# A recurrent attention loop: the attention mask copied into the score banks by ScalarE, and tail work moved within the tile

## The chip, the cores and the metric

The kernel runs on one core of one Trainium2 chip. It is one launch that computes a transformer block and its whole backward pass. The metric is the device time in microseconds (us). Three runs of the kernel before took 3000.04, 2988.55 and 2992.74 us, median 2992.74.

The engines are named as in the profile: PE (TensorE, matmuls and transposes), DVE (VectorE), ACT (ScalarE), POOL (GpSimd), SP (SyncE, which here issues most of the DMAs). L790 is line 790 of the kernel before. Matmul results land in PSUM; everything else lives in SBUF.

## The reference

The forward part, with a sequence of 2048 rows, D = 512, 32 heads of width 128, segments of 32 rows and a memory of 8 rows:

```python
mod = (silu(c) @ w_mod)                       # sa, ca, ga, sb, cb, gb
h = layernorm(x) * (1 + ca) + sa
mem = mem0
for s in range(64):                           # 64 segments
    hs = concat([mem, h[32*s : 32*s+32]])     # 8 + 32 = 40 rows
    q, k, v = hs @ Wq, hs @ Wk, hs @ Wv       # per head
    scores = q @ k.T * scale
    scores = where(mask, scores, -1e9)        # memory rows are seen by all, the rest is causal
    o = softmax(scores) @ v @ Wo
    mem = o[:8]                               # the next segment's memory
    outs.append(o[8:])
x = x + ga * concat(outs)
h = layernorm(x) * (1 + cb) + sb
out = x + gb * ((sigmoid(h @ w_gate) * (h @ w_up)) @ w_down)
```

The outputs are `out` and, for a given `grad_out`, the gradients of x, mem0, Wq, Wk, Wv, Wo, w_gate, w_up, w_down, c and w_mod. Because `mem` of one segment is an input of the next, the 64 segments can only run one after the other.

## The kernel before

The kernel has phases: a short phase 0 (modulation vectors, weights loaded), phase 2 (layernorm and the recurrent attention, from about 18.6 to 970 us), then the gated unit, the attention's backward pass and the weight gradients. The change touches phase 0 and phase 2 only, in the function `phase2` with its helpers.

**Tiling.** Four segments (s4 = 0, 1, 2, 3) make a tile of 128 rows; there are 16 tiles. The 40 rows of a segment are 8 memory rows and 24 rows in one 32-row block, and the remaining 8 rows, the *tail rows*. These do not need the memory to be projected, so the tail rows of all four segments are projected together, a tile ahead. Heads are kept in 11 groups of three (120 columns a group: 3 x 40). The groups are worked in three parts (`NP` = 3) of 4, 4 and 3 groups, that is 480, 480 and 360 columns.

**One segment**, in the order in which PE runs it:

1. Key and query passes of the 32-row block (`proj`, two halves each), value pass (`v_chunk`), with the transposes `turns` that bring rows to head columns.
2. `st_exp(0..2)`: the score matmuls of a part accumulate into a bank `st_ps` that already holds the mask (`start=False`); ScalarE's Exp (L850) reads it and writes ET. The mask is written there at the end of the segment before by `mask_mm` (L786, matmul at L790): a matmul of the identity with `maskT`, which has the mask already repeated for each group. There are three `st` banks, one for each part.
3. `den` (L854) and `recip` (L859) give the softmax's denominators; `pv` (L874) multiplies ET with the values into `or_ps`; `ost` scales the result into Ost: part 0 by VectorE in one instruction (L898), part 1 by ScalarE in four (L895), part 2 by VectorE.
4. `ott(0..2)`: transposes (L866) of Ost into `tps`, copied to OT (L61 ACT, L63 DVE): part 0 by VectorE, parts 1 and 2 by ScalarE.
5. `outproj` (`pair_mm`, L223): 64 matmuls of OT with Wo into `at_ps`, head pairs in order; `split_pair` (L230 ACT, L232 DVE) makes a high and a low bf16 half, `sum_pair` (L242) folds both into `at_ft`, and ScalarE copies the memory rows to `hT_next` (L1046). With that the next segment starts.

**Work laid into the segment.** The order of instructions on every engine in phase 2 is fixed as written: `pin(i0)` chains all instructions of an engine. So each `fill`, `p1`, `chunk` or `pop_later` call stands where it is called:

- `p1(j, k)`: step k of the layernorm of tile j, two tiles ahead: load L395, stats L398, scale L409, shift L414, turn L419. The turn is four transposes into `p1tp`, a copy by ScalarE (hx, L424) and one by GpSimd (hb, L426). Before: stats at the end of the projection of s4 = 0, scale at s4 = 1, shift at s4 = 2, turn at s4 = 3 between den(2) and pv(2).
- `b_pieces`: projection of the next tile's tail rows (`proj_b`, with stores `rows_out`), `turn_b` (L630, eight transposes, at the place "turn" of s4 = 2 for k and s4 = 3 for q, ahead of `ott(0)`). Its copies out of PSUM wait in the list `evacs` until `evac_turned`, after the output projection.
- `TailRows` (object `tail`): output projection of the tail rows of the tile before, 32 heads in pieces of sizes (24, 8), both at s4 = 3 after the projection (`ao_tps`, L215); then `split`, and at s4 = 0 of the next tile the fold (L327) with VectorE's cast `ao_b_tb` (L335), taken by `pop_later` (`early`).
- `store_rows`: for each segment the attention rows `at_ft` are cast (L335), transposed (`at_tp`, L339), copied (`at_rb`, L341) and stored (L345) in the next segment.

PSUM tiles named `or_ps`, `tps`, `turn_ps`, `p1tp`, `at_ps`, `at_tp`, `at_ft`, `ao_tps`, `pass_ps` share five buffers (tag "p").

**The first segment** is different: the weights arrive while it runs, and the output weights Wo come in quarters by SP (`load_wo`, L809). The stores of its rows (`first_stores`: 2 of RA0k, 6 of RBk, 6 of RBq, 2 of RA0q, L597 to L605) are issued by SP after the tail turn of q. Behind them SP issues the two DMA transposes VTr (L978, of the values) and Pst (L986, of ET), then OSR, OT. GpSimd normalizes Pst (L1062).

Of the kernel before, what the change touches and what calls it, by code (L numbers as in the profile page):

```python
# [7 lines left out]
BF16 = mybir.dt.bfloat16  # L8
F32 = mybir.dt.float32
# [31 lines left out]
class K:  # L41
# [336 lines left out]
    def phase1_setup(self, ctx, psum_tile_fn):  # L378
# [11 lines left out]
        def p1_tile(j):  # L390
# [28 lines left out]
            def turn():  # L419
                tp = psum_tile_fn()  # L420
                for c in range(DC):
                    nc.tensor.transpose(tp[:, c, :], st["h1"][:, c * 128:(c + 1) * 128], self.ident[:])
                hx = p1w.tile([128, DC, 128], BF16, name="hx", bufs=3)
                nc.scalar.activation(hx[:], tp[:, 0:DC, :], AF.Copy)  # L424
                hb = p1w.tile([128, DC, nseg, 8], BF16, name="hb", bufs=2)
                nc.gpsimd.tensor_copy(hb[:], hx[:].rearrange("p c (s t) -> p c s t", t=cfg.T)[:, :, :, 24:cfg.T])  # L426
                return hx, hb

# [12 lines left out]
    def phase2(self):  # L441
# [15 lines left out]
        with ExitStack() as ctx:  # L457
# [42 lines left out]

            def p1(j, k=None):
                if j < NT:
                    if j not in p1s:
                        p1s[j] = p1_tile(j)
                    for i in (range(1, 5) if k is None else [k]):
                        r = p1s[j][i]()
                        if r is not None:
                            hxs[j] = r

            p1s = {}  # L510
            mem0 = VTr[0:M, 0:DC, :].rearrange("m c x -> m (c x)")
            with tc.tile_pool(name="p0", bufs=1) as p0:
# [80 lines left out]

            def rows_out(rows, dram, s0, ns):

                if ns == 1:
                    nc.sync.dma_start(dram[s0, 0:96, 0:8, :].rearrange("r g e -> r (g e)"), rows[0:96, 0:1024])  # L597
                    nc.sync.dma_start(dram[s0, 0:96, 8:11, :].rearrange("(hl r) g e -> r hl (g e)", r=32),
                                      rows[96:128, :].rearrange("r (hl x) -> r hl x", hl=3))
                    return  # L600
                for j in range(3):
                    nc.sync.dma_start(dram[s0:s0 + 4, 96 + 8 * j:104 + 8 * j, 0:8, :].rearrange("s q g e -> s q (g e)"),
                                      rows[32 * j:32 * j + 32, 0:1024])
                for hl in range(3):
                    nc.sync.dma_start(dram[s0:s0 + 4, 96 + 8 * hl:104 + 8 * hl, 8:11, :].rearrange("s q g e -> s q (g e)"),  # L605
                                      rows[96:128, 384 * hl:384 * hl + 384])
# [4 lines left out]
            def b_pieces(t):  # L611
# [4 lines left out]
                def proj_b(x, a, n, eng):  # L616
                    hb = hxs[t][1]
                    self.col_pass(psp, Ws[x], 0, lambda c: hb[:, c, :, :].rearrange("p s q -> p (s q)"), RBt[x], eng, steps=(a, n))
                    if a + n == 8:
                        store = lambda: rows_out(RBt[x], DR[x], t * nseg_t, nseg_t)  # L620
                        if t == 0:
                            first_stores.append(store)
                        else:
                            store()

# [22 lines left out]
            def evac_turned():  # L648
                while evacs:
                    evacs.pop(0)()  # L650

            first_stores = []
            firsts = b_pieces(0)
# [127 lines left out]

            tail = TailRows(self, sb2, psp, psp, 1, "ao", rows_b, (24, 8), ptag="p")

            masked = {}

            def mask_mm(pi):  # L786

                n = min(PG, G - pi * PG)
                ps = masked[pi] = pst.tile([128, PG, GW], F32, name="st_ps", tag="st")
                nc.tensor.matmul(ps[:, 0:n, 0:120], lhsT=self.ident[:, :], rhs=maskT[:, 0:n, :], start=True, stop=False,  # L790
                                 skip_group_check=True)

            def tails_in(xs, s):
# [17 lines left out]
            for s in range(NS):  # L811
# [11 lines left out]
                def proj(x, hf, eng):  # L823
                    pass_half(x, hf, lambda c: hT[:, c, :], RA[x], eng)
                    if hf == 1 and s == 0:
                        first_stores.append(lambda: rows_out(RA[x], DR[x], s, 1))
                    elif hf == 1 and s < NS - 1:
                        rows_out(RA[x], DR[x], s, 1)
# [127 lines left out]
                if s == NS - 1:  # L956
# [28 lines left out]
                if s < NS - 1:  # L985
                    nc.sync.dma_start(Pst[:], ET[:, :], transpose=True)  # L986
                else:
                    nc.gpsimd.dma_start(self.w_up, io["B_w_up"].rearrange("(c p) f -> p c f", p=128))
# [1441 lines left out]
```

## Time and profile before

| | |
|---|---|
| runs | 3000.04, 2988.55, 2992.74 us; median 2992.74 |
| profiled execution | 2988.12 us, span 2986.3 us, mean granted PE clock 0.997 |
| busy | PE 2926.4 us (98%), DVE 1629.5, ACT 1270.7, POOL 1234.0 us |
| phase 2 | about 18.6 to 970 us |
| segment 0, segment 1 | 37.16 us, 17.68 us |
| a steady tile | 57.16 us: 14.25 (s4 = 0), 14.02 (1), 14.04 (2), 14.85 (3) |
| windows 300 to 500 us | PE 199.57 of 200 us, DVE 122.87, ACT 115.91, POOL 104.11, granted clock 1.00 |

A segment's length is the time from its first key matmul to that of the next. A PE row of the timeline covers several matmuls ("x7") and may overlap its neighbours, since matmuls are pipelined: the start of a row is the reliable number. "Idle before, releaser" tells what ended an engine's idle time. One granted clock value is the throttle's answer for a stretch: 1.00 is full speed.

### The profile page before, as it was taken

Reading aid. Unit: us, or ns where it says so; the run is one execution under the profiler, and the core shown is the slowest. Engines: PE = TensorE matmul, PEld = TensorE weight load, DVE = VectorE, ACT = ScalarE, POOL = GpSimd, SP = SyncE. Lnnn points to the kernel's source line nnn. Section 1 sums busy time; section 2 is a strip of 40 time slices with the busy share of each in tenths; the row PEclk is TensorE's granted clock in tenths of the full one; section 3 lists DMA queues with packets and bytes.
Section 4 is the critical chain, followed back from the end, with each engine's and each line's share of the span. In section 5 each row is a group of like instructions: output and inputs, shape, how many; then the busy total and the mean of one; then the engine's idle time right before and its main releaser. Section 6 shows DMA issues by size and latency. Waiting matters only on the chain.

```text
span 2986.3 us, 105797 instructions
## 1 busy us (share of the span) xinstructions
PE 2926.4 (98%) x43931; PEld 1837.4 (62%) x44005; DVE 1629.5 (55%) x3680; ACT 1270.7 (43%) x3055; POOL 1234.0 (41%) x2485
## 2 busy tenths in 40 slices
PE   6999999999999999999999999999999999999999
PEld 3666666666666544445577777777777754445455
DVE  5565666666655788833466665566566632840011
ACT  2555555555555533312355555555555520110011
POOL 2455555545555222221244444444444422762111
PEclk9999999999999999999999999999999999999999
DMA  9988889889889899988699999999999997886565
GB/s 307 222 217 218 211 216 224 211 220 215 208 217 274 211 233 231 230 280 281 205 249 251 251 254 246 250 254 249 251 254 252 248 282 246 253 261 191 159 216 171
DMA packets 837924, 703.04 MB, mean 235 GB/s; under 512 B 537682, under 2 KB 709890, under 8 KB 836548
## 3 DMA queue, kind: packets, MB, share of 16 engines
q1 hardware_dynamic: 711828, 485.29, 66.7%
q0 software_dynamic: 54512, 148.63, 15.6%
q10 hardware_dynamic: 71104, 62.34, 6.5%
q8 instruction: 346, 5.67, 0.8%
q14 instruction: 134, 1.10, 0.1%
HBM read 294.99 MB, written 276.35 MB: 191 GB/s over the span
## 4 chain that ended last, share of the span: by engine, by line
PE 91%; DMA 3%; DVE 2%; issue 1%; ACT 1%; SPq 0%; POOL 0%; DVEq 0%; ACTq 0%; POOLq 0%
PE pass_ps L257 14%; PE gps L2211 14%; PE dh_ps L215 8%; PE g_ps L1834 5%; PE pass_ps L666 5%; PE gps5o L2226 4%; PE dhq_ps L223 4%; PE at_ps L223 4%; PE mm L1315 3%; PE gps L1494 3%; PE dh_tps L215 3%; PE turn_ps L838 2%; PE mm L1275 2%; PE mm L1290 2%; PE tps L1751 1%; PE st_ps L848 1%
## 5 line engine op out<-in xcount | busy, mean ns | idle before, releaser
L2211 PE MATMUL gps<-rows,hrows 128*128 128x512 bf16 (+2 forms) x2124 | 413.6, 355 | 1.9
L2211 PEld LDWEIGHTS <-hrows 128*128 128x128 bf16 x2160 | 211.3, 98 | 204.3 <-issue 0.9
L63 DVE CAST ot<-gps 128x512 bf16<-128x512 f32 (+3 forms) x76 | 48.2, 634 | 309.8 <-PE gps L2211 230.4
L1062 POOL TENSOR_TENSOR Pst<-Pst,rden 120x1408 bf16<-120x1408 bf16 x63 | 159.9, 2537 | 116.9 <-issue 66.7
L1879 POOL COPY dOst<-RAd 96x512 bf16<-96x512 bf16 x128 | 75.3, 613 | 295.9 <-DVE RAd L63 295.9
L61 ACT ACTIVATE ot<-gps 128x512 bf16<-128x512 f32 (+3 forms) x75 | 41.2, 550 | 356.8 <-PE gps L2211 214.3
L666 PE MATMUL pass_ps<-Wv,hT 128*32 128x512 bf16 (+2 forms) x2304 | 186.8, 358 | 0.0
L2215 POOL DMA_DIRECT2D out_dram<-ot x104 | 78.7, 757 | 257.0 <-DVE ot L63 133.4
L257 PEld LDWEIGHTS <-hT 128*32 128x32 bf16 x4096 | 114.7, 97 | 98.3 <-issue 4.1
L63 DVE CAST Vst<-pass_ps 96x512 bf16<-96x512 f32 x128 | 87.2, 682 | 107.0 <-ACT RBv L61 98.1
L215 PE MATMUL dh_ps<-WvT,dVT 128*32 128x512 bf16 x2048 | 133.4, 380 | 1.6 <-DVE RBd L63 0.2
L666 PE MATMUL pass_ps<-Wv,hb 128*32 128x512 bf16 (+2 forms) x636 | 127.5, 347 | 2.1 <-DMA Wv<-in_A_Wv_dram 2.1
L223 PE MATMUL at_ps<-Wo,OT 128*32 128x256 bf16 x4096 | 124.7, 274 | 4.1 <-issue 2.1
L257 PE MATMUL pass_ps<-Wk,hT 128*32 128x512 bf16 x2048 | 123.2, 382 | 2.5 <-DVE mv L402 1.1
L257 PE MATMUL pass_ps<-WoT,dyT 128*32 128x256 bf16 (+1 forms) x3072 | 122.4, 308 | 0.9 <-ACT dyT L1960 0.9
L223 PE MATMUL dhq_ps<-WqT,dQT 128*32 128x256 bf16 x4096 | 122.9, 273 | 0.0
L257 PE MATMUL pass_ps<-Wq,hT 128*32 128x512 bf16 x2048 | 122.7, 379 | 0.0
L215 PE MATMUL dh_ps<-WkT,dKT 128*32 128x512 bf16 x2048 | 122.3, 380 | 0.0
L2226 PE MATMUL gps5o<-WoT,rows 128*128 128x512 bf16 x549 | 120.4, 379 | 1.4 <-DMA rows<-OSR 0.9
L801 POOL DMA_DIRECT2D Vst<-RBv x192 | 100.8, 530 | 47.7 <-ACT ET L850 30.7
L223 PEld LDWEIGHTS <-dQT 128*32 128x32 bf16 x4096 | 109.6, 97 | 15.8
L317 DVE TENSOR_TENSOR dST<-dh_ps,dST 128x512 bf16<-128x512 f32 x64 | 44.3, 692 | 130.3 <-ACT dST L316 130.3
(472 smaller groups left out, 7038.6 us busy)
## 6 DMA issues: line engine op xcount, KB each, us to landing
OSR<-Ost SPq DMA_DIRECT2D x64, 352.0 KB
OT<-OT SPq DMA_DIRECT2D x64, 352.0 KB
PS<-Pst SPq DMA_DIRECT2D x64, 352.0 KB
Pst_l<-PS SPq DMA_DIRECT2D x64, 352.0 KB
OT_l<-OT SPq DMA_DIRECT2D x64, 352.0 KB
DVR<-rows_x POOLq DMA_DIRECT2D x64, 352.0 KB, 6.4
DKR<-rows_x POOLq DMA_DIRECT2D x64, 352.0 KB, 5.7
DQR<-rows_x POOLq DMA_DIRECT2D x64, 352.0 KB, 3.5
```

The source lines that it names most:

```text
L63: return nc.vector.tensor_copy(out, in_)
L215: self.nc.tensor.matmul(ps[32 * j:32 * j + 32, :], lhsT=lhsT, rhs=w, start=(n < 4), stop=(n >= total - 4), tile_position=(0, 32 * j))
L223: nc.tensor.matmul(ps[32 * j:32 * j + 32, :], lhsT=x[k], rhs=w[k][:, 256 * d:256 * d + 256], start=(n == 0), stop=(n == total - 1), tile_p ...
L257: self.nc.tensor.matmul(ps[32 * j:32 * j + 32, :], lhsT=lhs(c), rhs=rhs, start=(c == 0), stop=(c == DC - 1), tile_position=(0, 32 * j))
L666: nc.tensor.matmul(ps[32 * j:32 * j + 32, o * E:(o + n) * E], lhsT=lhsT, rhs=wc[:, 3 * a + hl:3 * (a + n - 1) + hl + 1:3, :], start=(c == ...
L801: nc.gpsimd.dma_start(Vst[96 + 8 * j:104 + 8 * j, :], rb[32 * j + o:32 * j + o + 8, :])
L1062: nc.gpsimd.tensor_tensor(Pst[0:120, :, :], Pst[0:120, :, :], rden[:, :].unsqueeze(2).to_broadcast([120, G, 128]), op=ALU.mult)
L1315: nc.tensor.matmul(hp[:], lhsT=xT[:, fc, :], rhs=wT[:, fc, :], start=(n == 0), stop=(n == 2 * FC - 1))
L1494: nc.tensor.matmul(ps[:], lhsT=h2r[:, j, c * 128:(c + 1) * 128], rhs=xr[:, j, :], start=(j == 0), stop=(j == NT - 1))
L1834: nc.tensor.matmul(ps[:, j, 0:w], lhsT=lh[:, g * GW:(g + 1) * GW], rhs=rh[:, g * GW:g * GW + w], start=True, stop=True)
L2211: nc.tensor.matmul(ps[:, 0:ng * E], lhsT=hrows[:, tp_, c * 128:(c + 1) * 128], rhs=rows[:, tp_, 0:ng * E], start=(tp_ == 0), stop=(tp_ == ...
L2226: nc.tensor.matmul(pss[gg][:], lhsT=rows[:, t, gg * E:(gg + 1) * E], rhs=dyrows[:, t, :], start=(n == 0), stop=(n == NTP - 1))
```

## The change

- The mask of parts 0 and 1 is copied into the score banks by ScalarE (`mask_copy`), right after the copy to `hT_next`; part 2 by ScalarE in the next segment, behind the key pass's second copy. The first segment alone keeps `mask_mm`, now over the whole bank. The three `mask_mm` calls in each of the other segments go.
- The layernorm steps of a tile come a segment earlier: scale at s4 = 1 between the two query halves, shift at s4 = 1 after the projection, turn at s4 = 2 after `turn_b` and ahead of `ott(0)`. The two copies of the turn are put into `evacs` and run with `evac_turned` after the projection.
- `pop_later` (the early one, s4 = 0) goes from before `pv(2)` to after `ott(0)`.
- The tail pieces are (8, 16, 8) instead of (24, 8); the first 8 run at s4 = 3 between `ott(0)` and `ott(1)`.
- In the first segment `evac_turned` comes before the query turn; the 12 stores of the tail rows are issued by GpSimd, and the 4 stores of RA0k and RA0q by SP behind the Pst transpose.
- In phase 0 a one-element Exp (`e0`) is run by ScalarE.

```diff
 turn():
-                hx = p1w.tile([128, DC, 128], BF16, name="hx", bufs=3)
-                nc.scalar.activation(hx[:], tp[:, 0:DC, :], AF.Copy)
-                hb = p1w.tile([128, DC, nseg, 8], BF16, name="hb", bufs=2)
-                nc.gpsimd.tensor_copy(hb[:], hx[:]...[:, :, :, 24:cfg.T])
-                return hx, hb
+                def copies():
+                    (the same four lines)
+                    return hx, hb
+                return copies
...
 phase 0
+                nc.scalar.activation(p0.tile([1, 1], F32, name="e0")[:], self.sa_bc[0:1, 0:1], AF.Exp)
...
 proj_b, first tile
-                            first_stores.append(store)
+                            first_stores["b"].append(lambda: rows_out(RBt[x], DR[x], 0, nseg_t, nc.gpsimd))
...
-            tail = TailRows(self, sb2, psp, psp, 1, "ao", rows_b, (24, 8), ptag="p")
+            tail = TailRows(self, sb2, psp, psp, 1, "ao", rows_b, (8, 16, 8), ptag="p")
...
+            def mask_copy(pi):
+                n = min(PG, G - pi * PG)
+                ps = masked[pi] = pst.tile([128, PG, GW], F32, name="st_ps", tag="st")
+                nc.scalar.activation(ps[:, 0:n, 0:120], maskT[:, 0:n, :], AF.Copy)
...
                 proj("k", 1, "act")
+                if s > 0:
+                    mask_copy(2)
...
 first segment
+                    evac_turned()
                     turns((("q", "dve"),))
-                    evac_turned()
                     tails_in("q", 0)
-                    for f in first_stores:
+                    for f in first_stores["b"]:
                         f()
                 else:
                     proj("q", 0, "dve")
+                    if s4 == 1:
+                        p1(s // nseg_t + P1_AHEAD, 2)
                     proj("q", 1, "act")
...
                     nc.sync.dma_start(Pst[:], ET[:, :], transpose=True)
+                    if s == 0:
+                        for f in first_stores["a"]:
+                            f()
...
                 den(2, or2)
-                if s4 == 3:
-                    p1(s // nseg_t + P1_AHEAD, 4)
                 early = s4 == 0 and len(self.later) > 1
-                if early:
-                    self.pop_later()
-                more = list(range(NP)) if s + 1 < NS else []
-                if more:
-                    mask_mm(more.pop(0))
                 pv(2, or2)
                 recip(2, 3, or2)
                 ost(2, or2, "dve")
                 fill(s4, "turn")
+                if s4 == 2:
+                    p1(s // nseg_t + P1_AHEAD, 4, evacs)
...
-                if more and s4 < 2:
-                    mask_mm(more.pop(0))
                 ott(0)
-                if more:
-                    mask_mm(more.pop(0))
+                if s4 == 3:
+                    tail.chunk()
+                if early:
+                    self.pop_later()
                 ott(1)
                 ott(2)
...
                 evac_turned()
-                if s4 < 3:
-                    p1(s // nseg_t + P1_AHEAD, s4 + 1)
+                if s4 < 2:
+                    p1(s // nseg_t + P1_AHEAD, (1, 3)[s4])
...
-                ft = self.sum_pair(psp, parts, "at", "p", (lambda: mask_mm(more.pop(0))) if more else None)
+                ft = self.sum_pair(psp, parts, "at", "p")
                 if hT_next is not None:
                     nc.scalar.activation(hT_next[:, :, 0:M], ft[:, :, 0:M], AF.Copy)
+                    mask_copy(0)
+                    mask_copy(1)
```

More of the change, by code (lines that the diff above doesn't have):

```diff
@@ L422, in turn @@
                     nc.tensor.transpose(tp[:, c, :], st["h1"][:, c * 128:(c + 1) * 128], self.ident[:])
-                hx = p1w.tile([128, DC, 128], BF16, name="hx", bufs=3)
-                nc.scalar.activation(hx[:], tp[:, 0:DC, :], AF.Copy)
-                hb = p1w.tile([128, DC, nseg, 8], BF16, name="hb", bufs=2)
-                nc.gpsimd.tensor_copy(hb[:], hx[:].rearrange("p c (s t) -> p c s t", t=cfg.T)[:, :, :, 24:cfg.T])
-                return hx, hb
+                def copies():
+                    hx = p1w.tile([128, DC, 128], BF16, name="hx", bufs=3)
+                    nc.scalar.activation(hx[:], tp[:, 0:DC, :], AF.Copy)
+                    hb = p1w.tile([128, DC, nseg, 8], BF16, name="hb", bufs=2)
+                    nc.gpsimd.tensor_copy(hb[:], hx[:].rearrange("p c (s t) -> p c s t", t=cfg.T)[:, :, :, 24:cfg.T])
+                    return hx, hb
+                return copies
             return load, stats, scale, shift, turn
@@ L499, in phase2, with p1 @@
             hxs = {}
-            def p1(j, k=None):
+            def p1(j, k=None, defer=None):
                 if j < NT:
@@ L507, in p1 @@
                         if r is not None:
-                            hxs[j] = r
+                            if defer is None:
+                                hxs[j] = r()
+                            else:
+                                defer.append(lambda: hxs.update({j: r()}))
             p1s = {}
@@ L592, in to_heads, with rows_out @@
                 self.evac(eng, d[:, 0:2, b + 2 * w:b + 3 * w], s4[:, 6:8, 3, o:o + w])
-            def rows_out(rows, dram, s0, ns):
+            def rows_out(rows, dram, s0, ns, q=nc.sync):
                 if ns == 1:
@@ L601, in rows_out @@
                 for j in range(3):
-                    nc.sync.dma_start(dram[s0:s0 + 4, 96 + 8 * j:104 + 8 * j, 0:8, :].rearrange("s q g e -> s q (g e)"),
+                    q.dma_start(dram[s0:s0 + 4, 96 + 8 * j:104 + 8 * j, 0:8, :].rearrange("s q g e -> s q (g e)"),
                                       rows[32 * j:32 * j + 32, 0:1024])
                 for hl in range(3):
-                    nc.sync.dma_start(dram[s0:s0 + 4, 96 + 8 * hl:104 + 8 * hl, 8:11, :].rearrange("s q g e -> s q (g e)"),
+                    q.dma_start(dram[s0:s0 + 4, 96 + 8 * hl:104 + 8 * hl, 8:11, :].rearrange("s q g e -> s q (g e)"),
                                       rows[96:128, 384 * hl:384 * hl + 384])
@@ L650, in evac_turned @@
                     evacs.pop(0)()
-            first_stores = []
+            first_stores = {"a": [], "b": []}
             firsts = b_pieces(0)
@@ L789, in mask_mm @@
                 ps = masked[pi] = pst.tile([128, PG, GW], F32, name="st_ps", tag="st")
-                nc.tensor.matmul(ps[:, 0:n, 0:120], lhsT=self.ident[:, :], rhs=maskT[:, 0:n, :], start=True, stop=False,
+                nc.tensor.matmul(ps[:, :, 0:120], lhsT=self.ident[:, :], rhs=maskT[:, :, :], start=True, stop=False,
                                  skip_group_check=True)
+            def mask_copy(pi):
+                n = min(PG, G - pi * PG)
+                ps = masked[pi] = pst.tile([128, PG, GW], F32, name="st_ps", tag="st")
+                nc.scalar.activation(ps[:, 0:n, 0:120], maskT[:, 0:n, :], AF.Copy)
             def tails_in(xs, s):
@@ L825, in proj @@
                     if hf == 1 and s == 0:
-                        first_stores.append(lambda: rows_out(RA[x], DR[x], s, 1))
+                        first_stores["a"].append(lambda: rows_out(RA[x], DR[x], s, 1))
                     elif hf == 1 and s < NS - 1:
```

3 lines of the change are left out of this document (1 added, 2 removed).

## The prediction

> **What bounds the kernel now.** I read the page's busy shares and its chain first, then the windows of the forward loop, then the timeline of one tile, segment by segment.
>
> The page, busy time and chain:
>
> ```profile
> span 2986.3 us, 105797 instructions
> PE 2926.4 (98%) x43931; PEld 1837.4 (62%) x44005; DVE 1629.5 (55%) x3680; ACT 1270.7 (43%) x3055; POOL 1234.0 (41%) x2485
> PE 91%; DMA 3%; DVE 2%; issue 1%; ACT 1%; SPq 0%; POOL 0%; DVEq 0%; ACTq 0%; POOLq 0%
> ```
>
> PE decides. A busy PE is not a PE at its best, so taking matmuls out pays only where PE was issuing and not waiting for an operand. All edits lie in the forward attention loop (18.6 to 970 us). A tile there is four segments; between the first key matmuls of successive segments lie 14.25, 14.02, 14.04 and 14.85 us for s4 = 0, 1, 2, 3, 57.16 us a tile, the same to 0.02 us in most tiles. So I work segment by segment, on PE's timeline between the value pass and the output projection, where masks and transposes sit. At s4 = 1 (segment from 461.93; start and length in us, engine, line, operation, tiles, count):
>
> ```profile
> 470.59 0.36 PE L790 MATMUL st_ps<-maskT,ident 128*128 128x480 bf16 x1
> 470.79 0.33 PE L874 MATMUL or_ps<-Vst,ET 128*128 128x128 bf16 x3
> 470.96 0.37 PE L790 MATMUL st_ps<-maskT,ident 128*128 128x480 bf16 x1
> 471.30 0.38 PE L866 MATMUL tps<-ident,Ost 120*128 120x120 bf16 x4
> 471.52 0.32 PE L790 MATMUL st_ps<-maskT,ident 128*128 128x360 bf16 x1
> 471.68 0.64 PE L866 MATMUL tps<-ident,Ost 120*128 120x120 bf16 x7
> ...
> 470.55 0.69 DVE L898 TENSOR_TENSOR Ost<-or_ps,rden 120x512 bf16<-120x512 f32 x1
> ...
> 471.37 0.56 DVE L898 TENSOR_TENSOR Ost<-or_ps,rden 120x384 bf16<-120x384 f32 x1
> ```
>
> The reader should see that the first transposes (471.30) start 0.06 us after VectorE's Ost(0) ends (470.55 + 0.69 = 471.24), and the later ones wait for ScalarE's Ost(1) and VectorE's Ost(2) (471.93). The masks fill that wait. The same place at s4 = 2 (segment from 475.95):
>
> ```profile
> 485.43 0.38 PE L866 MATMUL tps<-ident,Ost 120*128 120x120 bf16 x4
> 485.64 0.37 PE L790 MATMUL st_ps<-maskT,ident 128*128 128x480 bf16 x1
> 485.84 0.53 PE L866 MATMUL tps<-ident,Ost 120*128 120x120 bf16 x7
> 486.36 1.82 PE L223 MATMUL at_ps<-Wo,OT 128*32 128x256 bf16 x60
> ...
> 484.72 1.14 ACT L895 ACTIVATE Ost<-or_ps,rden 120x128 bf16<-120x128 f32 x4
> ...
> 486.30 0.93 ACT L61 ACTIVATE OT<-tps 128x480 bf16<-128x480 bf16 x2 [0.44 <-issue]
> ```
>
> Here the output projection starts (486.36) while ScalarE has only begun its OT copy (486.30): its first heads need OT(0) alone.
>
> **The change, part by part.**
>
> Masks. Three L790 matmuls a segment leave PE, in 62 segments. Their issue slots by the rows (470.59 to 470.79; 471.52 to 471.68) are 0.20, 0.20 and 0.15 us, 0.55 together, so at most 62 x 0.55 = 34 us. At s4 = 1 all three lie in the waits named, so nothing comes back. At s4 = 0 they stand before the same waits; nothing by themselves. At s4 = 2 and 3 they come with the other moves and are counted there. In tiles 14 and 15, where no layernorm tile is left to prepare, s4 = 2 gains about 0.08.
>
> In their place ScalarE gets three PSUM copies. No row has ScalarE writing PSUM; the nearest is its OT copy of 480 columns (0.93 for two, 0.47 from one to the next, 0.57 for one alone). I take 0.57 each. Two stand behind the hT copy, when ScalarE is otherwise idle until the key pass ends some 2 us later; the third after the key evacuation, with the score matmuls 4 us away. They hold up only the tail's hi copy at s4 = 3: by about 0.5 us, to 2.14 us into the segment, against 2.59 when its buffer is wanted. Cost 0; free copies gain nothing either; at twice the price the slack is gone and about 0.5 us a tile is lost, 15 x 0.5 = +7. The ScalarE page of the Trainium skill ("ScalarE: Activation LUTs", Specifications) has a fixed cost plus one per element that makes 0.59 us for 480 columns, an estimate, and the sum stays as it is.
>
> Early fold at s4 = 0. VectorE's ao_b_tb cast (L335) goes from before to after ott(0):
>
> ```profile
> 456.91 0.44 DVE L335 CAST ao_b_tb<-ao_b_ft 128x128 bf16<-128x128 f32 x1
> ...
> 457.41 0.56 DVE L898 TENSOR_TENSOR Ost<-or_ps,rden 120x384 bf16<-120x384 f32 x1
> 457.88 0.40 DVE L63 COPY OT<-tps 128x480 bf16<-128x480 bf16 x1
> 458.34 1.17 PE L223 MATMUL at_ps<-Wo,OT 128*32 128x256 bf16 x36
> ```
>
> The cast takes 0.24 of VectorE's line (456.91 to 457.15) just ahead of recip, Ost(2) and OT(0), and with the masks gone too the projection comes 10.38 instead of 10.66 us into the segment: -0.28. The eight fold matmuls (0.20 us) then fall into the wait for Ost(1). Fourteen segments have it (8 to 60): -3.9, bounds 0 (the cast meets OT(0)) and 14 x 0.44 = -6.2.
>
> s4 = 2. The transposes of the layernorm tile (p1tp) come here, behind turn_b's, and the copies that empty both are behind the projection. The loop has five "p" PSUM buffers; three hold or_ps and now two are held. In the changed kernel's built order tps(1) takes or_ps(1)'s buffer and waits for all of ScalarE's Ost(1), and at_ps takes tps(1)'s: its first matmul waits for ScalarE's OT(1) copy, where before it waited for VectorE's OT(0). Worked out: Ost(1) ends 9.92 us into the segment; tps(1) 9.97 to 10.19; ScalarE's copy 10.44 to 11.01 (0.30 after the last transpose starts, 0.57 long); projection 11.07 instead of 10.41. That is +0.66, less 0.05 for the mask that stood between the hi and lo folds: +0.61, in 14 tiles +8.5 (bounds 0.55 and 0.70: +7.7 to +9.8). The four transposes (0.22) are hidden in this wait.
>
> s4 = 3. p1tp's 0.22 and the masks go; a tail chunk of 8 matmuls (0.43 us with the switches of tile shape) comes between ott(0) and ott(1), and the chunk behind the projection shrinks from 24 to 16. The new chunk's buffer is held too, so the projection waits for VectorE's at_rb copy, 11.2 to 11.3 instead of 10.79 us in; 8 matmuls fewer then win that back. -0.08 to +0.02 a tile; I take 0. Segment 3, without a chunk: -0.3. Moved scale and shift steps (0.54 and 0.69 on VectorE) and GpSimd's hb copy have idle time around them (1.69 us before the value evacuation); 0.
>
> Steady sum: +8.5 - 3.9 - 0.2 - 0.3 = +4.1.
>
> Start. Segment 1 takes 17.68 us, 3.65 over its kind. Rows of the timeline, and the window from 67 to 68 us:
>
> ```profile
> 65.07 1.40 ACT L850 ACTIVATE ET<-st_ps 128x480 bf16<-128x480 f32 x3 [2.90 <-DMA Pst<-ET]
> ...
> 61.35 1.39 SPq L986 DMA_TRANSPOSE Pst<-ET  x1
> ...
> 53.62 0.62 PE L223 MATMUL at_ps<-Wo,OT 128*32 128x256 bf16 x16 [0.72 <-DMA KST<-RA0k]
> ...
> 67.00:68.00 1.00, 1.00 (x10) 0.71 (x9) 0.96 (x3) 1.00 (x4) 1.00 (x2) 0.61 0.04 14
> ```
>
> The exp of segment 1 may not overwrite ET before segment 0's Pst transpose has read it, and that stands on SP behind 16 row stores (44.77 to 58.96). PE waits 2.1 us, and the clock then drops (0.61 in the last line's seventh column; 0.50 until 70.6), which costs 1.56. The change puts twelve stores on GpSimd's queue and four behind the transpose: -3.65. But segment 0's projection ends on the last Wo load (landing 53.6), and the twelve stores, issued about 0.55 us apart from 45.8 on, now run beside that load. From nothing to 1.7 us late; I take 1.0, nearer the middle as no row shows the two together. Net -2.65, bounds -3.65 and, if the stall comes back elsewhere as well, +1.7. GpSimd's next work, tails_in for segment 1, is then due at about 57, wanted at 62. The table load moved by e0 (1.28 us) had 0.74 of idle behind it: 0.
>
> Sum: +4.1 - 2.65 = +1.5. The profiled execution took 2988.12 us, 4.6 below the median of 2992.74; I put the sum on the median: 2994.2.
>
> **Rivals.**
>
> Buffers do not bind (faster). If at s4 = 2 the projection needed no buffer of ScalarE's, that segment would lose three masks and win four transposes: -0.33; s4 = 3 -0.08, s4 = 0 -0.28; 14 x -0.69 = -9.7, with -0.5 and -2.65: 2992.74 - 12.8 = 2980. Were every mask slot to come back as well, 2956. Against it: the waits at 471.30, and five buffers that the order fills. The Trainium skill ("Perfetto Trace Analysis", Optimization Strategy) says that gaps which repeat on the engine that should be full can mean too little PSUM for the next tile; by that rule I keep the +0.61.
>
> The clock (slower). If the new 0.66 us wait, each tile, tipped PE to half clock as after segment 1, each would cost about the 1.7 us of that window: 14 x 1.7 = +24 and 3018. It decides from the point where one drop follows a wait this short. Against: PE idled 2.14 us at 257.04 and the clock stayed at 1.00. [...]
>
> The start does not get shorter: the stores delay the Wo load by 1.7 us and the stall returns: +5.8, 2998.5. For it: the projection already waits for that load. ScalarE at twice the price, +7, gives 3001.
>
> **How the numbers follow.** Forecast 0.58; buffers do not bind 0.20, of which 0.08 goes beyond -15 us; start not shorter or ScalarE dear 0.12; clock or another wait on that scale 0.10. About 0.5%, 15 us, is what a measurement of this kernel can tell from no change. Faster 0.09, same 0.79, slower 0.12. The range takes in the first rival and the dear copies with the spread of the runs (2988.55 to 3000.04): 2978 to 3007.
>
> **What would show it.** Tile length near 57.5 instead of 57.16; s4 = 0 about 13.97, s4 = 1 unchanged, s4 = 2 about 14.65, s4 = 3 about 14.85; at s4 = 2 the first at_ps matmul behind ScalarE's OT copy; segment 1 about 14; ScalarE's copies into st_ps near 0.57. Wrong if s4 = 2 gets shorter, if s4 = 1 gains, or if the granted clock falls below 1 inside the tiles.

## The result, and the profile after

Over 22 runs of each, the changed kernel takes 2996.40 us in the median and the kernel before 2989.68 us: ratio 1.0023, 95% interval 1.0017 to 1.0030. That is 6.7 us more, small but clear of no change. One run of the changed kernel took 3696.04 us at a granted clock of 0.752 and stands outside ratio and interval.

The page of the changed kernel, span and busy time:

```profile
span 2998.1 us, 105333 instructions
PE 2908.9 (97%) x43742; PEld 1825.3 (61%) x43816; DVE 1642.9 (55%) x3680; ACT 1349.4 (45%) x3245; POOL 1239.1 (41%) x2497
```

and its window from 300 to 500 us (columns: length, busy time of PE, PEld, DVE, ACT, POOL, granted clock, DMA share, GB/s):

```profile
300.00:500.00 200.00, 194.07 (x3885) 130.49 (x3878) 122.72 (x287) 132.84 (x350) 103.20 (x210) 1.00 0.85 215
```

In the window PE was busy for 199.57 of 200 us before; now it is for 194.07. The masks did leave PE, and PE idles for what they took: a tile is not shorter but 0.29 us longer. Segment lengths, medians of the steady tiles, in us:

| kernel | s4 = 0 | 1 | 2 | 3 | tile |
|---|---|---|---|---|---|
| before | 14.25 | 14.01 | 14.04 | 14.85 | 57.15 |
| changed | 13.90 | 14.19 | 14.52 | 14.83 | 57.44 |
| forecast | 13.97 | 14.02 | 14.65 | 14.85 | 57.5 |

Segment s4 = 2 (from 531.88), to be read against the fence of the prediction at the same place:

```profile
541.15 0.39 PE L422 MATMUL p1tp<-ident,h 128*128 128x128 bf16 x4
541.37 0.95 PE L879 MATMUL tps<-ident,Ost 120*128 120x120 bf16 x11
542.30 0.22 PE L339 MATMUL at_tp<-ident,at_tb 128*128 128x128 bf16 x1
542.88 1.93 PE L223 MATMUL at_ps<-Wo,OT 128*32 128x256 bf16 x64 [0.36 <-ACT OT L61]
...
540.60 1.14 ACT L908 ACTIVATE Ost<-or_ps,rden 120x128 bf16<-120x128 f32 x4
542.25 0.93 ACT L61 ACTIVATE OT<-tps 128x480 bf16<-128x480 bf16 x2 [0.51 <-issue]
543.07 0.60 ACT L61 ACTIVATE b_colsk<-turn_ps 128x512 bf16<-128x512 bf16 x1
543.55 0.62 ACT L426 ACTIVATE hx<-p1tp 128x512 bf16<-128x512 bf16 x1
```

The projection (542.88) is now released by ScalarE's OT copy: it starts 11.00 us into the segment, against 10.41 before. The copy that would free p1tp's buffer (hx) comes only at 543.55.

Segment s4 = 0 (from 561.41), VectorE and PE:

```profile
570.85 0.56 DVE L911 TENSOR_TENSOR Ost<-or_ps,rden 120x384 bf16<-120x384 f32 x1
571.32 0.40 DVE L63 COPY OT<-tps 128x480 bf16<-128x480 bf16 x1
571.63 0.44 DVE L335 CAST ao_b_tb<-ao_b_ft 128x128 bf16<-128x128 f32 x1
...
571.78 1.49 PE L223 MATMUL at_ps<-Wo,OT 128*32 128x256 bf16 x47
```

The cast now stands behind OT(0), and the projection starts 10.37 into the segment instead of 10.66, as worked out.

Where the profiled execution's 11.8 us more (2998.1 against 2986.3) lie, all but 0.2 of them:

| stretch | before | changed | difference |
|---|---|---|---|
| start to segment 2's first key matmul | 73.43 | 72.12 | -1.3 |
| segments 2 to 62 | 873.68 | 875.90 | +2.2 |
| seam: segment 63 to the unit's first w_downT matmul | 33.99 | 38.56 | +4.6 |
| the rest, to PE's last matmul; same instructions in both | 2001.66 | 2007.72 | +6.1 |

Segments 2 to 62 hold one segment of 16.44 us (14) in the execution before, 2.4 over its kind, and none like it in the other, so the tiles themselves give about 15 x 0.29 = +4.4. The rest took between 2000.5 and 2012.5 us over the 13 profiles of this study, with the same instructions in each kernel; a +6.1 within that scatter can't be put down to the change. What is left for the change by this profile: -1.3 + 4.4 + 4.6 = +7.7, near the +6.7 of the medians.

### The profile page after: what moved, and what is told of

Same layout as the page of the kernel before. It is cut to its first block, busy times and chain, and to the rows that moved or that the text cites. A ratio compares the mean times of both kernels' runs of the same rounds, so it can differ in the third digit from the quotient of the medians.

```text
span 2998.1 us, 105333 instructions
## 1 busy us (share of the span) xinstructions
PE 2908.9 (97%) x43742; PEld 1825.3 (61%) x43816; DVE 1642.9 (55%) x3680; ACT 1349.4 (45%) x3245; POOL 1239.1 (41%) x2497
## 4 chain that ended last, share of the span: by engine, by line
PE 67%; DMA 2%; issue 1%; DVE 1%; ACT 1%; POOL 0%; DVEq 0%; SPq 0%; POOLq 0%; ACTq 0%
PE gps L2228 14%; PE dh_ps L215 8%; PE pass_ps L257 6%; PE g_ps L1851 5%; PE gps5o L2243 4%; PE dhq_ps L223 4%; PE mm L1332 3%; PE dh_tps L215 3%; PE gps L1511 3%; PE mm L1292 2%; PE mm L1307 2%; PE tps L1768 1%; PE mm L1261 1%; PE gps L1410 1%; PE mm L1265 1%
## 5 line engine op out<-in xcount | busy, mean ns | idle before, releaser
L223 PE MATMUL at_ps<-Wo,OT 128*32 128x256 bf16 x4096 | 124.5, 274 | 14.5 <-ACT OT L61 5.8
L223 PEld LDWEIGHTS <-OT 128*32 128x32 bf16 x4096 | 106.8, 97 | 24.5 <-issue 13.4
L345 POOL DMA_DIRECT2D AOA<-at_rb x64 | 36.3, 567 | 202.9 <-DVE at_rb L341 202.9
```

The lines of the kernel that those rows point to most:

```text
L223: nc.tensor.matmul(ps[32 * j:32 * j + 32, :], lhsT=x[k], rhs=w[k][:, 256 * d:256 * d + 256], start=(n == 0), stop=(n == total - 1), tile_p ...
```

## The experiments

**The masks alone.** The kernel before, with the mask matmuls replaced as in the change (the edit in short):

```diff
-                    mask_mm(more.pop(0))        # three places
+                    mask_copy(0); mask_copy(1)  # behind the hT copy
+                    mask_copy(2)                # behind the key pass's second copy
```

> The kernel before with one edit: the masks are copied by ScalarE, nothing else is moved. If the mask matmuls filled waits (my theory), s4 = 0 and 1 stay at 14.25 and 14.02 us within 0.03; s4 = 2 loses 0.05 to 0.10 (the third mask stood between the hi and the lo fold); s4 = 3, where the first mask stands in a stretch that PE itself sets, loses 0.2 to 0.35. Tile 57.16 -> 56.7 to 56.9, 15 tiles: -4 to -7 us against the kernel before. If every issue slot came back, each segment would lose 0.55: tile 54.96, -34 us. If ScalarE's copies into PSUM cost anything, s4 = 0 or 1 get longer and the whole is not faster; then the change's loss is the mask's and not that of the moved work.

Measured: s4 = 0 to 3: 14.19, 13.95, 13.90, 14.61, tile 56.65, 0.50 less than before; ratio 0.9974 (0.9958 to 0.9991), faster by about 8 us. ScalarE's rows:

```profile
513.11 1.06 ACT L797 ACTIVATE st_ps<-maskT 128x480 f32<-128x480 bf16 x2
...
515.81 0.47 ACT L797 ACTIVATE st_ps<-maskT 128x360 f32<-128x360 bf16 x1
```

The copies cost what the OT copy did (two in 1.06 us; 0.47 for 360 columns) and hold up nothing. By size, they took 0.568 us for 480 columns and 0.470 for 360. Of 0.55 us of mask slots in a segment, 0.06, 0.06, 0.14 and 0.24 come back: the rest had filled waits. So a longer tile is not the masks' doing by themselves. It must come from the moves, or from the two together.

**The moves alone.** The changed kernel with the mask matmuls put back.

> The changed kernel with the mask matmuls back where they were, no mask copies: the moves alone. If masks and moves add up, its tile is 57.44 + 0.51 = 57.95 us; s4 = 0 13.96, s4 = 1 14.26, s4 = 2 14.66, s4 = 3 15.07. If the longer waits at s4 = 2 and 3 now hide the masks as well, s4 = 2 and 3 are as in the changed kernel, within 0.1 (14.52 to 14.62, 14.83 to 14.93), and the masks' removal is worth less there than alone.

Measured: 14.10, 13.98, 14.83, 15.28, tile 58.19 (its one run took 3008.86 us): 1.04 over the kernel before, and 0.75 over the changed one. The moves cost a microsecond a tile. They and the masks do not simply add (that would be 57.94): at s4 = 2 and 3 the mask matmuls lengthen the moved order by 0.31 and 0.45, more than the 0.14 and 0.24 that they cost in the order before, so they are not hidden in the new waits; at s4 = 0 it is 0.20 against 0.06; at s4 = 1, on the other hand, the moves alone lose nothing, while the changed kernel loses 0.18. That is taken up below.

**The turn's copies at once.**

```diff
-                    p1(s // nseg_t + P1_AHEAD, 4, evacs)
+                    p1(s // nseg_t + P1_AHEAD, 4)
```

> The changed kernel, but the two copies that empty p1tp are made at once and not put off behind the output projection. All instructions are the same, only ScalarE's hx copy comes 1.4 us earlier. If the held PSUM buffer makes the projection wait for ScalarE's OT(1) copy (my theory), the projection at s4 = 2 starts about 10.5 to 10.6 us into the segment instead of 11.00, and s4 = 2 goes from 14.52 to 14.05 to 14.15. If the loss at s4 = 2 came from ScalarE's mask copies or from the four transposes on PE, it stays at 14.5, or grows, as the hx copy now stands ahead of OT(1) on ScalarE. Other segments unchanged.

Measured: s4 = 2 14.08, the others as in the changed kernel (13.90, 14.18, 14.83). PE and ScalarE at s4 = 2 (segment from 528.20):

```profile
537.70 0.95 PE L879 MATMUL tps<-ident,Ost 120*128 120x120 bf16 x11
538.61 0.22 PE L339 MATMUL at_tp<-ident,at_tb 128*128 128x128 bf16 x1
538.75 0.72 PE L223 MATMUL at_ps<-Wo,OT 128*32 128x256 bf16 x17
...
537.94 0.61 ACT L426 ACTIVATE hx<-p1tp 128x512 bf16<-128x512 bf16 x1
538.57 0.93 ACT L61 ACTIVATE OT<-tps 128x480 bf16<-128x480 bf16 x2
```

The projection (538.75, 10.55 into the segment) starts before ScalarE's OT(1) copy has ended, though that copy begins 10.37 into the segment as in the changed kernel. The same instructions on every engine, ScalarE's hx copy 1.9 us earlier in the segment (9.74 against 11.67): 0.44 us a segment. The held buffer is shown as the cause of the loss at s4 = 2.

**The scale step behind the projection.**

```diff
-                    if s4 == 1:
-                        p1(s // nseg_t + P1_AHEAD, 2)     # between the query halves
...
-                if s4 < 2:
-                    p1(s // nseg_t + P1_AHEAD, (1, 3)[s4])
+                for k in ((1,), (2, 3), (), ())[s4]:
+                    p1(s // nseg_t + P1_AHEAD, k)
```

> The changed kernel, but the layernorm's scale step (two VectorE instructions) is made with the shift step behind the projection of s4 = 1, not between the query halves. In the changed kernel the first of them (L411) takes 1.47 us at s4 = 1, while GpSimd multiplies Pst, against 0.54 in the kernel before, and the value evacuation behind it starts 0.35 later. If that is the loss at s4 = 1 (theory: VectorE's L411 is slowed by GpSimd's work beside it), L411 goes back to 0.54 and s4 = 1 from 14.19 to 13.95 to 14.05. If the loss comes from the mask copies on ScalarE, L411's place changes nothing and s4 = 1 stays at 14.19.

Measured: s4 = 1 13.95, 0.24 less; the others as in the changed kernel. The scale instruction over all tiles (least, median and longest in ns), first of the changed kernel:

```profile
L411 DVE TENSOR_SCALAR xh<-x,mv,rstd x16: 541/1475/2085, 7.0 to 809.6; 128x512 f32<-128x512 bf16 x16
```

and of this one:

```profile
L411 DVE TENSOR_SCALAR xh<-x,mv,rstd x16: 536/540/547, 7.1 to 810.8; 128x512 f32<-128x512 bf16 x16
```

What stands beside it in the changed kernel at s4 = 1 (segment from 517.69):

```profile
519.75 2.55 POOL L1079 TENSOR_TENSOR Pst<-Pst,rden 120x1408 bf16<-120x1408 bf16 x1
...
521.12 1.47 DVE L411 TENSOR_SCALAR xh<-x,mv,rstd 128x512 f32<-128x512 bf16 x1
522.63 0.69 DVE L412 TENSOR_TENSOR xh<-xh,ca_bc 128x512 f32<-128x512 f32 x1
523.24 0.68 DVE L63 CAST Vst<-pass_ps 96x512 bf16<-96x512 f32 x1
```

and in the kernel with the moves alone (segment from 524.51):

```profile
526.08 2.54 POOL L1082 TENSOR_TENSOR Pst<-Pst,rden 120x1408 bf16<-120x1408 bf16 x1
...
527.95 0.95 DVE L411 TENSOR_SCALAR xh<-x,mv,rstd 128x512 f32<-128x512 bf16 x1
```

In both L411 ends 0.28 to 0.29 us after GpSimd's multiplication of Pst ends (522.59 against 522.30; 528.90 against 528.62), whenever it began. Over the 14 tiles of each of these two kernels it is 0.28 to 0.30 every time. Where the multiplication begins later still, L411 grows with it: 2.70 us into segment 49 of the changed kernel, L411 takes 2.09 and the segment 14.80. In the changed kernel the multiplication begins half a microsecond later in the segment (2.06 instead of 1.57): ahead of it GpSimd stores a row that ScalarE copies (L205), and that copy now stands behind the two mask copies (0.74 against 0.21 into the segment). So L411 takes 1.47 instead of 0.95, and the value evacuation behind it is late by 0.35. This is the one place where the mask copies on ScalarE do cost something, by way of GpSimd and VectorE.

Two more rows bear on this. The moves alone are not safe from it: in five of their 14 tiles the multiplication begins 1.88 to 2.49 us into the segment, and s4 = 1 takes 14.08 to 14.69. And in the next experiment's kernel the multiplication of segments 5 and 9 begins only after L411, which then takes 0.54 at this same place, and the segments take 13.83 and 13.88: what costs is the overlap, not the place.

**The tail pieces of before.**

```diff
-            tail = TailRows(self, sb2, psp, psp, 1, "ao", rows_b, (8, 16, 8), ptag="p")
+            tail = TailRows(self, sb2, psp, psp, 1, "ao", rows_b, (24, 8), ptag="p")
...
-                if s4 == 3:
-                    tail.chunk()          # between ott(0) and ott(1)
```

> The changed kernel with the tail pieces (24, 8) of before, so no chunk between the transposes at s4 = 3. If that chunk's PSUM buffer makes the projection wait for at_rb (my theory), the projection at s4 = 3 starts near 10.65 us into the segment instead of 11.49, and 24 instead of 16 tail matmuls behind it give back 0.45: s4 = 3 from 14.83 to 14.5 to 14.6. If the chunk were worth its place (it fills a wait), s4 = 3 becomes longer, 15.0 to 15.3.

Measured: s4 = 3 14.43 instead of 14.83, a little below the expected 14.5; the others unchanged. PE in the changed kernel (segment from 546.39):

```profile
556.42 0.61 PE L215 MATMUL ao_tps<-Wo,ao_tail 128*32 128x512 bf16 x8
556.97 0.54 PE L879 MATMUL tps<-ident,Ost 120*128 120x120 bf16 x7
557.35 0.22 PE L339 MATMUL at_tp<-ident,at_tb 128*128 128x128 bf16 x1
557.89 1.82 PE L223 MATMUL at_ps<-Wo,OT 128*32 128x256 bf16 x60 [0.32 <-DVE at_rb L341]
```

and here (segment from 543.10):

```profile
553.66 0.22 PE L339 MATMUL at_tp<-ident,at_tb 128*128 128x128 bf16 x1
553.82 1.93 PE L223 MATMUL at_ps<-Wo,OT 128*32 128x256 bf16 x64
```

The projection starts 10.72 into the segment instead of 11.50. Of these 0.78, 0.40 is the chunk's own time on PE (the at_tp transpose comes at 10.56 instead of 10.96), and the rest the wait for at_rb, which is gone; 16 instead of 24 tail matmuls behind the projection had won back about half. Net 0.40 us a tile. That the wait came from the chunk's held buffer is argued from the order of the buffers; no run keeps the chunk and frees its buffer.

**The start's edits alone.** The kernel before, with the tail-row stores on GpSimd, four row stores behind the Pst transpose, evac_turned ahead of the query turn, and the one-element Exp:

> The kernel before with the start's edits alone: evac_turned ahead of the query turn, twelve tail-row stores on GpSimd, four row stores behind the Pst transpose, the one-element Exp. All steady tiles stay 57.16 us. Start: if the stores beside the last Wo load delay it, segment 0 is 38.0 to 39.4 (before: 37.16) and segment 1 14.0 to 14.3 (before: 17.68), together -1 to -3 us. Seam: in the changed kernel and the three kernels run from it, GpSimd's last row store at about 970 us waits 2.8 to 3.6 us where the kernel before and the one with the masks alone have 0.3 to 0.6, and the unit behind starts 2 to 4.6 us later. If the twelve more GpSimd stores, 900 us earlier, cause this (they shift which of the eight store slots each later store has), it shows here too, and the whole is no faster than before: -2 to +3 us. If it comes from the moved tail work, the wait here is 0.3 to 0.6 and the whole is -1 to -3 us.

Measured: tiles 57.14; segments 0 and 1 38.78 and 13.93, to segment 2 71.22 instead of 73.43; ratio 1.0009 (1.0000 to 1.0019). The start gains 2.2 us, the seam is 2.4 longer, with the long wait on GpSimd, and the whole is not faster. GpSimd at the seam, in the kernel before, with PE behind it:

```profile
972.32 0.99 POOL L779 DMA_DIRECT2D AOA<-ao_b_rb  x2 [0.86 <-DMA Wv<-in_B_w_down_dram]
973.85 0.50 POOL L779 DMA_DIRECT2D AOA<-ao_b_rb  x1 [0.55 <-DMA AOA<-at_rb]
...
974.94 0.58 POOL L1188 TENSOR_TENSOR rstd<-ve,mhalf 128x1 f32<-128x1 f32 x1 [0.48 <-DVE ve L1185]
...
979.03 0.55 PE L1153 MATMUL tp<-ident,Wv 128*128 128x128 bf16 x7 [0.59 <-DVE w_downT L63]
```

and in the changed kernel:

```profile
974.30 0.99 POOL L786 DMA_DIRECT2D AOA<-ao_b_rb  x2 [1.73 <-DMA Wv<-in_B_w_down_dram]
978.12 0.50 POOL L786 DMA_DIRECT2D AOA<-ao_b_rb  x1 [2.83 <-issue]
...
978.81 0.58 POOL L1205 TENSOR_TENSOR rstd<-ve,mhalf 128x1 f32<-128x1 f32 x1
...
982.90 0.37 PE L1170 MATMUL tp<-ident,Wv 128*128 128x128 bf16 x2 [4.83 <-DVE w_downT L63]
```

The last of nine row stores waits for the landing of the first of them (at_rb; both signal the same semaphore, one of eight that take turns). In the kernel before it is issued 0.28 us after that landing. In the changed kernel at_rb, issued at 969.32, has landed by the trace at 974.90, 5.6 us later (5.4 before), and yet the last store is issued only at 978.12: not the landing is late, but GpSimd, by 3.2 us, and the profile names nothing that it waits for ("issue"). GpSimd's rstd (a layernorm's factor for each row) stands behind it, VectorE's layernorm behind that, and behind the layernorm the w_downT copies that PE waits for: 4.83 us, where the same wait was 0.59 before. Behind the wait PE ran at half clock as well (0.50 from 982.91 to 986.32): from the end of the wait to the first w_downT matmul it took 3.68 us instead of 2.06. So of the seam's +4.6, 2.95 is the later rstd and 1.6 the clock. In the start's edits alone the wait was 2.79, the clock 1.00, and the seam has the 2.4 of the later rstd alone. (Of the seven kernels with the long wait on GpSimd, four have waits of 3.80 to 4.83 us here, with half clock behind them, and three of 2.47 to 2.90, with full clock.) The stores, their number and their order at this place are the same in both kernels.

**The mended kernel, with six, none, four, eight and twelve stores on GpSimd.** The three edits above together (turn's copies at once, scale later, pieces (24, 8)), and the twelve stores of the first tile divided between GpSimd and SP. All five keep the rest of the change.

```diff
-  first_stores["b"].append(lambda: rows_out(RBt[x], DR[x], 0, nseg_t, nc.gpsimd))
+  first_stores["b"].append(lambda: rows_out(RBt[x], DR[x], 0, nseg_t, nc.gpsimd if x == "k" else nc.sync))
...
                     nc.sync.dma_start(Pst[:], ET[:, :], transpose=True)
                     if s == 0:
-                        for f in first_stores["a"]:
+                        for f in first_stores["a"] + first_stores["b"]:
```

> The changed kernel with four things mended: the turn's copies at once, the scale step behind the projection, tail pieces (24, 8), and the six query tail-row stores on SP behind the Pst transpose (six key stores stay on GpSimd). By the single runs: s4 = 0 13.90, s4 = 1 13.95, s4 = 2 14.08, s4 = 3 14.43, tile 56.36, against 57.16 before and 56.65 with the masks alone: 15 x 0.80 = -12 us in the tiles, start -2 to -4 us, seam 0 to +4: in all -10 to -16 us, 2974 to 2980. If the single gains overlap, the tile is longer than 56.5 and the kernel no better than with the masks alone. Start: if the GpSimd stores' traffic delays Wo, half of it gone lets segment 0 end 1 to 2 us earlier than in the changed kernel (37 to 38 us).

> As the one before, but the six key stores are on SP too, ahead of the VTr transpose, so that GpSimd issues as many stores as in the kernel before. Tiles as there (56.36). Seam: if the number of GpSimd stores at the start decides it, the last store's wait is back to 0.3 to 0.6 us and the unit starts 2 to 4 us earlier than with twelve; if the moved tail work decides, the wait is 2.8 or more again. Start: the Pst transpose of segment 0 comes up to 4 us later; if segment 1's exp is then again the one that waits, segment 1 is 15 to 17 us, else about 14.

> The mended kernel of the run with six GpSimd stores, but four of the twelve stores of the first tile's tail rows on GpSimd, eight on SP. Tiles unchanged at 56.35 us. The wait of GpSimd's last row store at about 960 us was 2.8 to 3.6 us in the six kernels with twelve such stores, and absent in those with none or six. GpSimd's stores go through eight slots in turn: twelve shift the turn by four, six by six, none by none. If the slot's number decides, four stores give the long wait again (2.8 us or more, seam 36 us or more, from the last segment's start to the unit's first L1275 matmul); if it is rather the number or the traffic of the stores, the wait is gone here (seam about 34).

> The same with eight of the twelve stores on GpSimd, four on SP. Eight shift the turn of the slots by nothing. If the slot's number decides, no long wait (seam about 34 us); if more than six stores bring it, the wait is 2.8 us or more (seam 36 or more).

> The mended kernel with all twelve tail-row stores on GpSimd as in the changed kernel: the turn's copies at once, scale behind the projection, pieces (24, 8). Tile 56.35. The slot theory fell with four stores (no long wait). If twelve stores bring the long wait whatever the tile looks like, it is here: 2.8 us or more, seam 36 us or more. If it takes the unmended moves together with the stores, or if it follows the moment at which the last stores meet the other transfers, it is not: seam about 34.

Measured: all five have 13.90, 13.95, 14.08, 14.43, tile 56.35, so the three gains add up in full. Six stores: 2974.28 us, ratio 0.9955 (0.9940 to 0.9969); none: 2978.71, ratio 0.9974 (0.9963 to 0.9984), against the kernel before. The one with six stores beats both kernels of this case; with four, eight and twelve one run each took 2981.15, 2975.83 and 2978.77 (the single runs of the three gains by themselves: 2991.84, 2988.78, 2990.05). For the seam I use the time from segment 63's start to GpSimd's rstd:

| stores of the first tile on GpSimd | kernels | start of rstd, us |
|---|---|---|
| none | before; masks alone; mended | 27.83; 27.14; 28.12 |
| 4, 6, 8 | mended | 27.77; 27.95; 27.97 |
| 12 | changed; turn; scale; pieces; start alone; moves alone; mended | 30.78; 30.52; 29.94; 30.04; 30.22; 30.47; 30.14 |

The last store at the seam, with eight and with twelve:

```profile
959.28 0.50 POOL L786 DMA_DIRECT2D AOA<-ao_b_rb  x1 [0.15 <-issue]
```

```profile
960.52 0.50 POOL L786 DMA_DIRECT2D AOA<-ao_b_rb  x1 [3.81 <-issue]
```

With twelve stores at 45 us the last store at the seam is issued 3.21 us after at_rb has landed, in seven kernels of seven; with none to eight, 0.28 to 0.54 us after, in six of six. My explanation by the slot's number falls: four stores shift the slots as twelve do, and have no long wait. But such a hold is not found with twelve stores only. The kernel before has one too, on another row store, inside a tile:

```profile
705.15 1.50 POOL L779 DMA_DIRECT2D AOA<-ao_b_rb  x3 [2.83 <-issue]
```

The masks alone and the mended kernel without such stores have the same 2.83 us on the same store, the 250th DMA that GpSimd issues, at 697.63 and 694.47. PE does not wait for it: the segments around it are as long as their kind. In the seven kernels with twelve stores none shows ahead of the seam, and the 371st DMA has it, which is the last store at the seam, where rstd stands behind. That twelve stores put a hold there, and eight do not, is shown, with the rest of the kernel the same; that they move the one of the kernel before fits, but is not shown; what the hold is, and what sets its place, stays open.

The start's times scatter: to segment 2 70.3 to 73.4 us with twelve stores (seven profiles), 71.1 with six, 73.2 with none, 71.1 and 72.0 with four and eight. Fewer GpSimd stores did not bring the last Wo load earlier (last projection matmuls at 53.93 with six, 55.54 with none, 54.46 in the changed kernel), so that these stores delay it is not shown.

## Why the prediction was right, and where its steps were wrong

The forecast of 2994.2 and its +1.5 us lie near the measured 2996.4; but +6.7 is more than four times +1.5. The time came out near partly by luck: the median it was put on, 2992.74, lay 3.1 above the later 2989.68, and in the steady part of the sum (+4.1, measured about +4.4) the cost missed at s4 = 1 is cancelled by smaller misses at the other three. The 15 us that the prediction took as the least to be told from no change were too many: 22 runs of each told 6.7. Point by point:

- *The masks fill waits.* Right. Alone they give 0.50 us a tile of their 2.2; PE's busy time fell by 5.5 us in 200 and the tile grew. The price taken for the copies, 0.57, was measured as 0.568 for the two of 480 columns (median of 126); the third, of 360, takes 0.470. 189 matmuls left PE, so 63 segments and not 62. The rule that the prediction draws from the Trainium skill ("ScalarE: Activation LUTs") stands there under "What ACT_TABLE_LOAD costs", not under Specifications; its estimate of 0.59 for 480 columns agrees within 0.02.
- *s4 = 0, -0.28.* Right in mechanism, -0.35 measured; 0.06 of the difference is what the masks alone bring there.
- *s4 = 2, +0.61.* Right: +0.48, by the wait that was named (at_ps for ScalarE's OT(1) copy), and shown by making the copy earlier. Oversized by 0.13: ScalarE's copy began 10.37 into the segment where I had 10.44, so the projection came at 11.00 and not 11.07; and of the 0.59 that it is later, 0.11 came back behind it, where I had 0.05.
- *s4 = 3, 0.* Right as a net, -0.02, made of the two parts that were named. But the projection came at 11.50, later than the 11.2 to 11.3 of the prediction. That net hid a choice: without the new chunk it is 0.40 shorter.
- *Scale and shift "have idle time around them; 0".* Wrong: +0.18 at s4 = 1, 2.5 us over 14 tiles. I gave L411 the 0.54 us of its row behind the projection; between the query halves, beside GpSimd's multiplication, it took 1.47. The idle time was there, the duration was not the same in it. The Trainium skill ("SBUF — State Buffer", Who interferes with whom) has the rule: VectorE's second port pair is GpSimd's too, and a VectorE instruction that uses it is blocked for as long as a GpSimd instruction holds it. The trace agrees: L411 ends 0.28 to 0.30 us after the multiplication in all 28 places, at different beginnings of it.
- *The start, -2.65.* Right in direction, oversized: -1.3 in this profile, -2.2 in the start's edits alone. Segment 1 lost 3.38 of the 3.65; but segment 0 was 1.7 us longer, not 1.0, and began 0.4 later. The last Wo quarter came only 0.8 later (54.46 against 53.62; the row of the kernel before names KST<-RA0k as what ended the wait, and that it was Wo is the prediction's reading); PE had waited 1.01 and 3.06 us for Wo, and ran on at half clock:

```profile
54.46 1.04 PE L223 MATMUL at_ps<-Wo,OT 128*32 128x256 bf16 x16 [3.06 <-DMA Wo<-in_A_Wo_dram]
55.29 1.92 PE L257 MATMUL pass_ps<-Wk,hb 128*32 128x512 bf16 x16
```

  The windows of the same stretch (the clock is the seventh column):

```profile
50.00:52.00 2.00, 0.72 (x16) 0.34 (x15) 0.00 (x0) 0.00 (x0) 1.74 (x3) 0.77 1.17 362
52.00:54.00 2.00, 0.00 (x0) 0.00 (x0) 0.00 (x0) 0.00 (x0) 1.98 (x7) 0.50 1.18 165
54.00:56.00 2.00, 1.54 (x24) 0.93 (x28) 0.02 (x1) 0.39 (x1) 0.94 (x5) 0.50 1.89 123
```

  The sixteen key matmuls took 1.92 us at a clock of 0.50, against 1.04 before: 0.9. The attention of segment 0 was earlier than before (projection from 48.61, not 51.41), so PE waited longer for the same load. The drop itself came before the longest wait: a mean of 0.77 from 50 to 52 puts it at about 51.1, with only the waits of 0.84 (at 48.61) and 1.01 us behind it. In the 3.4 us ahead of it PE was busy for 1.56 us; in the kernel before, the drop at 67.2 came after 3.4 us with 1.33 us of work, and the single wait of 2.14 us at 257.04 was followed by none. So here the length of the single wait alone does not tell whether the clock falls. I had priced the load, and not the clock.
- *The seam.* Missing from the sum: no term for anything behind segment 63, as the instructions there are the same. It is the largest miss, +4.6 in this profile: the later rstd, which the start's edits alone bring too (+2.4), and half clock behind the longer wait (1.6).
- *The rivals.* The buffers did bind, against the first. The clock did not fall inside the tiles (1.00 in the window shown), against the second; it fell at the start and at the seam. The third, a start that is not shorter, did not hold, but the start's gain was lost elsewhere, at the seam.

## What to carry to other kernels

A step moved into a wait is free only if what it holds is free too: here 0.22 us of transposes in a wait cost 0.48, because their PSUM buffer stayed taken until after the next matmul group's start; ask when the buffer is emptied, not only when the engine is idle. Its duration belongs to the new place, not to the old row: look at what the neighbour engine does there. And put several moves on the chip one at a time: the masks alone gave 0.26%, and the moves made with them took that back, while the mended moves gave 0.45% together with them.

## What the runs showed of the hardware that was not expected

A VectorE tensor_scalar of 128x512 (0.54 us alone) takes 0.95, 1.47 and up to 2.09 us beside a GpSimd tensor_tensor of 2.55 us, ending 0.28 to 0.30 us behind it. GpSimd held one of its stores for about 3 us with nothing to wait for, in ten of the kernels here: the 250th DMA that it issued, or, with twelve more stores at 45 us, the 371st, 900 us on, where it cost 2.4 to 3 us; the cause is open. The clock fell to 0.50 behind 3.4 us in which PE was busy for 1.56 us and waited for no longer than 1.01 us at a time.
